# First 46 chunks of a gated recurrence scanned channel-major through TensorE transposes, all token loads issued by SyncE

## The chip, the cores and the metric

The kernel runs on one core of a Trainium2 chip. The metric is device time in microseconds (us), the median of its runs. Five engines work side by side, each through its own instructions in order: TensorE (PE, matmuls), VectorE (DVE), ScalarE (ACT), GpSimd (POOL) and SyncE (SP). SP, ACT and POOL also issue DMA transfers from their instruction streams; an engine whose next instruction is a transfer that must wait stands still until that wait is over. Sixteen DMA engines carry the transfers.

## The reference

Two stages follow each other. The first is a recurrence over 5056 time steps for 4 batch rows and 256 channels; the second sends each of the 20224 resulting rows (tokens) through one of 8 experts, chosen by a hash of the token's id.

```python
f = lower_bound + (1.0 - lower_bound) * sigmoid(f_logit)
i = 1.0 - f
for t in range(S):                       # S = 5056
    h = f[:, t] * h + i[:, t] * x[:, t]  # per batch row and channel
    y[:, t] = h
expert_idx = token_ids * 2654435761 % 8
for e in range(8):
    out[expert_idx == e] = relu(y[expert_idx == e] @ w1[e]) @ w2[e]   # 256 -> 1024 -> 256
```

## The kernel before, in words

**Chunks and blocks.** Time is cut into 158 chunks of 32 steps; a chunk holds 4 x 32 = 128 tokens. Chunks are grouped into 17 blocks (`NGS`: 2, 2, 4, eleven blocks of 12, then 8, 6, 4). For each block the program loads `f_t` and `x_t` (time on partitions, 256 channels along the row, 8 transfers, half of them issued by SP and half by ACT, line 479), takes the sigmoid (ACT, L503), turns both tiles with VectorE's 32x32 transpose so that time runs along the row (L530, tiles `sT` and `xT`), applies `lower_bound` (the gate, ACT, L544), forms the input term (DVE, L556), scans (DVE, L569, tile `y`) and turns the result back (DVE, L587, tile `yT`). A scan of one block starts from the last column of the block before.

**Routing.** A rank stage at the start computes for every token a place in a DRAM buffer `srt`, in which each expert has a contiguous region of 21 x 128 rows. GpSimd writes each chunk's 128 rows to their places by one indirect transfer (the scatter, L601): 158 scatters. GpSimd's transfers of the 16 weight tiles (L456, L458) stand among them.

**Experts.** 168 tiles of 128 rows (21 per expert) are read back turned (`xe`, an SP transfer, L680), multiplied by w1 (PE, 16 matmuls, L689), passed through relu (ACT, L698), multiplied by w2 (PE, 8 matmuls, L707), copied out of PSUM in pairs (ACT, L715, tile `ob`) and written to their token rows by an indirect GpSimd transfer (the out, L721): 168 outs. A tile may be read once every chunk that can hold one of its rows has been scattered. `window` bounds that from the statistics of the hash: 8 tiles become ready after block 3 (20 chunks), the last 8 after the last block. `Tab` (L620 to L659, DVE and PE) inverts the places into row numbers, which the outs need.

**What sets the order.** Nothing is scheduled on the chip. A planner in the program (`Plan`) gives each task an engine, a cost, a priority and dependencies, and emits a list; each engine then runs its part of the list in that order. Its priorities are due times in chunks (`due[k] = 6 + 2.3 * G0[k]`), a tile's is its last block's due time plus 30. A transfer issued by SP or ACT is given one of eight completion semaphores in turn (the names DMAHW0 to DMAHW7 in listings of the order), and before it is issued the engine waits until the transfer that had this semaphore before has landed, whichever queue that one is in. GpSimd's transfers have eight of their own (DMASW).

Of the kernel before, what the change touches and what calls it, by code (L numbers as in the profile page):

```python
# [15 lines left out]
P = 128  # L16
E = 8
# [27 lines left out]
class Task:  # L45
    def __init__(self, name, eng, prio, emit, deps=(), alloc=None, use=(), dma=0.0, lat=0.0, alt=False):
# [3 lines left out]
        self.done = None  # L50


class Plan:


    SEM = 0.12

# [13 lines left out]
    def order(self):  # L71
# [13 lines left out]
        def at(t):  # L85
            r = base[t]
# [11 lines left out]
        while left:  # L98
# [3 lines left out]
            for e in free:  # L102
# [25 lines left out]
            for c in kids.get(t, ()):  # L128
                base[c] = max(base.get(c, 0.0), t.done + self.SEM)
# [7 lines left out]
def kernel(  # L137
# [48 lines left out]
    ld = main.enter_context(tc.tile_pool(name="ld", bufs=2))  # L186
    sc = main.enter_context(tc.tile_pool(name="sc", bufs=2))
# [37 lines left out]
    def init_pool():  # L225
        nc.gpsimd.iota(i32a[:], pattern=[[1, NT]], base=0, channel_multiplier=0)
# [628 lines left out]
```

## Time and profile before

| | us |
|---|---|
| median of 2 runs | 620.59 (620.12 to 621.06) |
| span on the profile's page | 619.1 |
| a profiled execution as recorded: whole / its core's span | 616.68 / 614.9 |
| busy: PE, DVE, ACT, POOL | 348.5, 346.7, 321.1, 373.5 |
| HBM read and written | 58.49 MB, 33.95 MB |

Busy time is the time in which an engine executes; a GpSimd indirect transfer is counted while GpSimd makes it, not while it is under way. The two executions in the table differ: the one recorded took 1.8 us more than its core's span; with the same 1.8 us around it, the one on the page took 620.9 us. The trace is read by views: the page's summary, the waits of an engine, groups by line, stretches of time, and the timeline of one engine.

### The profile page before, as it was taken

The numbers are of one execution on the slowest core, as the hardware profiler recorded it, in microseconds if no ns is written. First come the engines' busy times: TensorE is split into PE (matmuls) and PEld (weight loads), VectorE is DVE, ScalarE is ACT, GpSimd is POOL, SyncE is SP. The second block draws the span as 40 slices with busy tenths as digits, with TensorE's granted clock in tenths as the row PEclk, the third lists the DMA queues.
The fourth block names the chain that finished last, engine by engine and source line by source line (L and its number), as shares of the span: only waits on it lengthen the run. The fifth ranks groups of instructions, "written<-read, shape, count | busy, mean of one in ns | idle before, by whom it ended". The sixth has DMA issues, their size and how long they took to land.

```text
span 619.1 us, 11412 instructions
## 1 busy us (share of the span) xinstructions
PE 348.5 (56%) x4258; PEld 320.1 (52%) x4258; DVE 346.7 (56%) x597; ACT 321.1 (52%) x431; POOL 373.5 (60%) x393
## 2 busy tenths in 40 slices
PE   2100005603696526289649975149870598986792
PEld 1000005503596426279638964149760597976792
DVE  8977989833993339988402777549539333110000
ACT  1333433703694517569418955058681377755372
POOL 6234374771277573887826776728777367776353
PEclk9999999956799758789968978559985598999697
DMA  8999999974048947843998387252883335333241
GB/s 154 274 264 288 231 230 154 261 209 90 26 121 200 291 97 143 214 95 109 207 231 187 90 174 138 64 102 79 195 214 96 89 92 153 113 105 95 80 100 54
DMA packets 116527, 94.58 MB, mean 153 GB/s; under 512 B 57133, under 2 KB 106801, under 8 KB 116468
## 3 DMA queue, kind: packets, MB, share of 16 engines
q0 software_dynamic: 23664, 39.61, 27.2%
q1 hardware_dynamic: 71114, 33.40, 24.3%
q10 hardware_dynamic: 21690, 20.79, 14.7%
q8 instruction: 35, 0.57, 0.4%
q14 instruction: 24, 0.20, 0.1%
HBM read 58.49 MB, written 33.95 MB: 149 GB/s over the span
## 4 chain that ended last, share of the span: by engine, by line
PE 27%; issue 24%; POOL 17%; DMA 16%; DVE 9%; ACT 4%; SPq 1%; ACTq 1%; POOLq 0%; DVEq 0%
PE hp L689 14%; PE op L707 13%; POOL srt L601 9%; POOL out_dram L721 8%; DMA xe<-srt 8%; DMA srt<-yT,pos_i 4%; DMA x_t<-in_x_dram 3%; ACT hT L698 2%; DVE y L569 2%; DVE xT L556 1%; DVE xT L530 1%; DVE sT L530 1%; ACT sT L544 1%; SPq L680 1%; DVE A L620 1%
## 5 line engine op out<-in xcount | busy, mean ns | idle before, releaser
L721 POOL DMA_INDIRECT out_dram<-ob,row_i x168 | 182.9, 1089 | 138.5 <-ACT ob L715 92.7
L689 PE MATMUL hp<-xe,w 128*128 128x128 bf16 x2688 | 197.6, 234 | 77.5 <-DMA xe<-srt 77.5
L601 POOL DMA_INDIRECT srt<-yT,pos_i x158 | 172.1, 1089 | 97.6 <-issue 44.8
L689 PEld LDWEIGHTS <-w 128*128 128x128 bf16 x2688 | 184.4, 106 | 84.4 <-issue 68.5
L698 ACT ACTIVATE hT<-hp 128x1024 bf16<-128x1024 f32 x168 | 170.2, 1022 | 110.9 <-PE hp L689 68.7
L707 PE MATMUL op<-w,hT 128*128 128x256 bf16 x1344 | 184.1, 285 | 64.1 <-ACT hT L698 63.9
L707 PEld LDWEIGHTS <-hT 128*128 128x128 bf16 x1344 | 129.4, 102 | 83.9 <-ACT hT L698 67.4
L544 ACT ACTIVATE sT<-sT,lb_col,c_col 128x384 f32<-128x384 f32 (+4 forms) x136 | 79.6, 629 | 117.3 <-DMA xe<-srt 56.0
L569 DVE TENSOR_TENSOR_SCAN y<-sT,y,xT 128x384 bf16<-128x384 f32 (+4 forms) x128 | 103.0, 845 | 0.5
L556 DVE SCALAR_TENSOR_TENSOR xT<-sT,xT 128x768 f32<-128x768 f32 (+2 forms) x58 | 50.0, 865 | 84.3 <-ACT sT L544 82.7
L530 DVE STREAM_TRANSPOSE xT<-x_t 128x768 f32<-128x768 f32 (+3 forms) x64 | 51.0, 808 | 46.9 <-DMA x_t<-in_x_dram 46.9
L640 PE MATMUL tp<-BP,A 128*128 128x64 bf16 (+4 forms) x158 | 9.4, 216 | 105.4 <-DVE BP L631 101.7
L503 ACT ACTIVATE f_t<-f_t 128x1024 f32<-128x1024 f32 (+1 forms) x41 | 40.3, 1017 | 51.8 <-DMA xe<-srt 25.0
L640 PEld LDWEIGHTS <-A 128*128 128x128 bf16 x158 | 8.4, 112 | 106.4 <-DVE A L620 80.0
L530 DVE STREAM_TRANSPOSE sT<-f_t 128x768 f32<-128x768 f32 (+3 forms) x64 | 50.7, 804 | 20.0 <-ACT f_t L503 18.2
L715 ACT COPY ob<-op 128x512 f32<-128x512 f32 x84 | 48.9, 582 | 5.0 <-PE op L707 4.9
L587 DVE STREAM_TRANSPOSE yT<-y 128x384 f32<-128x384 f32 (+4 forms) x68 | 30.3, 462 | 20.3 <-DMA srt<-yT,pos_i 20.0
L620 DVE TENSOR_TENSOR A<-iota_lo,lo_h 128x1536 bf16<-128x1536 bf16 (+4 forms) x17 | 23.4, 1374 | 0.0
L647 DVE TENSOR_TENSOR Tab<-Tab,tp 128x64 f32<-128x64 f32 (+4 forms) x17 | 3.3, 193 | 25.3 <-PE tp L640 25.1
L357 PE MATMUL rps<-cumI,onesb 128*128 128x8 bf16 (+2 forms) x24 | 3.7, 225 | 12.9 <-DVE cumI L342 12.3
L628 DVE TENSOR_TENSOR BP<-BP,v 128x384 bf16<-128x384 bf16 (+6 forms) x17 | 8.0, 472 | 0.6
L631 DVE TENSOR_TENSOR BP<-BP,v 128x384 bf16<-128x384 bf16 (+6 forms) x17 | 8.0, 471 | 0.6
(73 smaller groups left out, 81.0 us busy)
## 6 DMA issues: line engine op xcount, KB each, us to landing
f_t<-in_f_logit_dram SPq DMA_DIRECT2D x22, 384.0 KB
f_t<-in_f_logit_dram ACTq DMA_DIRECT2D x22, 384.0 KB
x_t<-in_x_dram ACTq DMA_DIRECT2D x22, 384.0 KB
x_t<-in_x_dram SPq DMA_DIRECT2D x22, 384.0 KB
w<-in_moe_w_dram POOLq DMA_DIRECT2D x16, 512.0 KB
xe<-srt SPq DMA_TRANSPOSE x168
out_dram<-ob,row_i POOLq DMA_INDIRECT x168
srt<-yT,pos_i POOLq DMA_INDIRECT x158
```

The lines of the kernel that those rows point to most:

```text
L503: nc.scalar.activation(v, v, AF.Sigmoid)
L530: nc.vector.transpose(o, i_)
L544: nc.scalar.activation(v, v, AF.Identity, scale=c_col[:, c:c + 1], bias=lb_col[:, c:c + 1])
L556: nc.vector.scalar_tensor_tensor(x_.rearrange("p s c l -> p (s c l)"), f_.rearrange("p s c l -> p (s c l)"), 1.0, x_.rearrange("p s c l -> ...
L569: nc.vector.tensor_tensor_scan(timed(T["y", k][:, cp, :L, s]), timed(T["sT", k, u][:, s, n, :]), timed(T["xT", k, u][:, s, n, :]), init, o ...
L587: nc.vector.transpose(T["yT", k].bitcast(FP32).rearrange("p m (c j) -> p c m j", j=32)[:, cp, :ng, :], T["y", k][:, cp, :L, :].rearrange(" ...
L601: bi = nc.gpsimd.indirect_dma_start(out=srt[:], out_offset=bass.IndirectOffsetOnAxis(ap=pos_i[:, g:g + 1], axis=0), in_=T["yT", k][:, m, : ...
L689: nc.tensor.matmul(hp[:, f, :], lhsT=w1_sb[e][:, h, f * P:(f + 1) * P], rhs=xe[:, h, :], start=(h == 0), stop=(h == 1),)
L698: nc.scalar.activation(hT[:], T["hp", j, e][:], AF.Relu)
L707: nc.tensor.matmul(op[:, h, :], lhsT=T["hT", j, e][:, f, :], rhs=w2_sb[e][:, f, :], start=(f == 0), stop=(f == FF - 1),)
L715: nc.scalar.copy(ob[:], T["op", n // 2][:])
L721: bi = nc.gpsimd.indirect_dma_start(out=out, out_offset=bass.IndirectOffsetOnAxis(ap=row_i[:, c:c + 1], axis=0), in_=T["ob", n // 2][:, h, ...
```

## The change

- **Blocks.** 24 blocks instead of 17: 2, 4, five of 8 chunks, then 4, 4, twelve of 8, 4, 2, 2 (`TS` in steps).
- **First 7 blocks (46 chunks) channel-major.** A load puts 128 tokens on partitions with 256 channels along the row, for a 256-step block two consecutive steps per partition. TensorE turns 128 x 128 pieces of `f_t` and `x_t` (float32, by an identity matrix) into PSUM, so that channels are on partitions; ACT takes the sigmoid from PSUM, then the gate; DVE forms the input term with `x` out of PSUM and scans; TensorE turns `y` (bfloat16) back and ACT copies it into `yT`. There are 184 float32 and 92 bfloat16 transposes of 128 x 128. No VectorE transposes are left in these blocks.
- **The other 112 chunks** keep the 32x32 layout. The state passes from one layout to the other by four matmuls and two VectorE instructions (`hand_pe`, `hand_dve`).
- **Queues.** All loads of `f_t` and `x_t` are issued by SP; ACT issues four loads of ids at the start only. Three blocks of loads are held instead of two (`XF`).
- **Weights** are released to GpSimd's order one every 4 us of the plan.
- **PSUM.** Two buffers instead of three for the first product (`hp`), four instead of two for the rest (`op`).
- **Planner.** It may take a task of better priority that becomes ready shortly after another (`LOOK`), the tables are due 25 later (`TABD`), the tiles are spread between blocks (`OFF`, `pace`).

The core of the diff:

```diff
-NGS = [2, 2, 4] + [12] * 11 + [8, 6, 4]
+TS = [64, 128] + [256] * 5 + [128, 128] + [256] * 12 + [128, 64, 64]
+KS = 7
+NGS = [t // 32 for t in TS]
-MID = 80
-RANGES = [(0, 8), (8, MID), (MID, NG)]
+RANGES = [(0, 6), (6, GA), (GA, MID), (MID, NG)]
+XF = 3
+OFF, TABD = 20.0, 25.0
+W0, W1 = 8.0, 4.0
...
+    LOOK = {"PE": 0.3, "ACT": 0.3, "DVE": 0.5, "POOL": 0.1, "SP": 0.1}
...
-                t = min((m[1] for m in mine if m[0] <= s + 1e-9), key=lambda t: t.prio)
+                s, t = min((m for m in mine if m[0] <= s + self.LOOK[e]), key=lambda m: (m[1].prio, m[0]))
...
-    pl.pool("hp", 3)
-    pl.pool("op", 2)
+    pl.pool("hp", 2)
+    pl.pool("op", 4)
...
-            weights.append(add(f"w{e}{v}", {"POOL": 0.85}, 14 + 2 * e + v, wl,
-                               [weights[-2]] if len(weights) >= 2 else [], dma=2.8, lat=2.0))
+            weights.append(add(f"w{e}{v}", {"POOL": 0.85}, 5, wl, rel=W0 + W1 * (2 * e + v), dma=2.8, lat=2.0))
...
+                nc.sync.dma_start(
+                    t[:, 2 * q * half:2 * q * half + 2 * q, :].rearrange("p (b r) d -> p b (r d)", r=q),
+                    src[2 * half:2 * half + 2].rearrange("b (p r) d -> p b (r d)", r=q),
+                )
...
+                    for n, view in enumerate(cview):
+                        nc.tensor.transpose(view(t), T[which, k][:, u * nch + n, h * P:(h + 1) * P], idf[:])
...
+                    nc.scalar.activation(
+                        T["sT", un][:, h * HS:h * HS + cols], T["tr", "f", uh][:, :cols], AF.Sigmoid
+                    )
...
+                        nc.tensor.transpose(t[:, n, h * P:(h + 1) * P], src, idn[:])
...
+            nc.tensor.matmul(
+                hp[:, c, :], lhsT=rep4[:, c].rearrange("p b j -> p (b j)"), rhs=last_y, start=True, stop=True
+            )
...
-            for b in (0, 2, 1, 3):
-                on_sp = b < 2
+            for b in range(B):
                 task = add(
-                    f"ld{t}{k}.{b}", {"SP": 0.45} if on_sp else {"ACT": 0.43}, pr - 12 if k > 1 else pr - 100,
-                    lambda t=t, b=b, q=nc.sync if on_sp else nc.scalar, f=load: f(t, b, q),
+                    f"ld{t}{k}.{b}", {"SP": 0.45}, pr - 22,
+                    lambda t=t, b=b, f=load: f(t, b, nc.sync),
...
-        pr = due[k] + 4
+        pr = due[k] + TABD
...
-        pr = due[lb] + 30 + 0.01 * n
+        mine = [i for i, t in enumerate(seq) if t[0] == lb]
+        pace = 2.3 * NGS[min(lb + 1, NB - 1)] / len(mine)
+        pr = due[lb] + 2.3 * NGS[lb] + OFF + pace * (n - mine[0])
```

**Order on ACT, the program before, around the loads of block 7 (chunks 56 to 67).** `f_t_1097` and `x_t_1096` are that block's loads, `sT` the gates of block 6; the brackets name what a row waits for.

```order
L503 ACTIVATE f_t_708<-f_t_708 128x1024 x2
L479 DMA f_t_1097<-in_f_logit_dram 32x12x256 [waits DMAHW4_49]
L479 DMA f_t_1097<-in_f_logit_dram 32x12x256 [waits DMAHW6_49]
L479 DMA x_t_1096<-in_x_dram 32x12x256 [waits DMAHW4_49,DVE_49]
L479 DMA x_t_1096<-in_x_dram 32x12x256 [waits DMAHW3_49]
L544 ACTIVATE sT_1136<-sT_1136,lb_col_86,c_col_87 128x384 [waits DVE_49]
```

On ACT in the changed program, where loads and sigmoids of the 32x32 blocks follow each other, at the sigmoid of block 10 (`hT` is a relu, `ob` a copy of a finished pair of tiles):

```order
L953 ACTIVATE hT_2106<-hp_2075 128x1024 [waits PE_49,Activation_49]
L797 ACTIVATE sT_2052<-sT_2052,lb_c_86,c_c_87 128x256
L756 ACTIVATE f_t_1653<-f_t_1653 128x1024 [waits DMAHW4_49,DMAHW5_49,DMAHW3_49,DMAHW2_49]
L970 COPY ob_2152<-op_2108 128x512 [waits DMASW7_49,DMASW6_49,PE_49]
L953 ACTIVATE hT_2174<-hp_2134 128x1024 [waits PE_49,Activation_49]
```

The transfers are gone from ACT; a wait on a DMAHW semaphore stands only before an instruction that uses what was loaded.

**Order on POOL in the program before, at the scatters of block 7 (`yT_1637`) and block 8 (`yT_2231`).** `srt<-yT` is a scatter, `out<-ob` an out, x11 a run of eleven.

```order
L601 DMA srt_79<-yT_1637,pos_i_88 21504x256 x10
L721 DMA out_0_dram<-ob_2369,row_i_90 20224x256 x2
L601 DMA srt_79<-yT_1637,pos_i_88 21504x256
L721 DMA out_0_dram<-ob_2440,row_i_90 20224x256 x2
L721 DMA out_0_dram<-ob_2516,row_i_90 20224x256 x2
L601 DMA srt_79<-yT_1637,pos_i_88 21504x256
L721 DMA out_0_dram<-ob_2574,row_i_90 20224x256 x2
L601 DMA srt_79<-yT_2231,pos_i_88 21504x256 x11
L721 DMA out_0_dram<-ob_2757,row_i_90 20224x256 x2
```

And in the changed program, at its blocks 13 (`yT_3569`) and 14 (`yT_3904`):

```order
L537 DMA srt_79<-yT_3569,pos_i_90 21504x256 x2
L976 DMA out_0_dram<-ob_4319,row_i_92 20224x256 x2
L537 DMA srt_79<-yT_3569,pos_i_90 21504x256
L976 DMA out_0_dram<-ob_4401,row_i_92 20224x256 x2
L537 DMA srt_79<-yT_3569,pos_i_90 21504x256
L537 DMA srt_79<-yT_3904,pos_i_90 21504x256
L976 DMA out_0_dram<-ob_4489,row_i_92 20224x256 x2
```

Runs of 10 to 16 scatters have become runs of one or two between pairs of outs; two longer runs are left, 24 before the first out and 11 near the end.

**Order on SP in the program before, at the end of the loads of block 7 and the tile reads (`xe`) behind them.**

```order
L479 DMA x_t_1096<-in_x_dram 32x12x256 [waits DMAHW5_49]
L680 DMA_TRANSPOSE xe_1179<-srt_79 128x2x128 [waits DMAHW7_49,DMASW7_49,PE_49]
L680 DMA_TRANSPOSE xe_1188<-srt_79 128x2x128 [waits DMAHW0_49,DMASW0_49,PE_49]
L680 DMA_TRANSPOSE xe_1197<-srt_79 128x2x128 [waits DMAHW1_49,DMASW1_49,PE_49]
L680 DMA_TRANSPOSE xe_1222<-srt_79 128x2x128 [waits DMAHW2_49,DMASW2_49,PE_49]
L680 DMA_TRANSPOSE xe_1246<-srt_79 128x2x128 [waits DMAHW3_49,DMASW3_49,PE_49]
```

And in the changed program, at the loads of block 12 (chunks 78 to 85):

```order
L935 DMA_TRANSPOSE xe_2182<-srt_79 128x2x128 [waits DMAHW5_49,PE_49]
L733 DMA f_t_2197<-in_f_logit_dram 32x8x256 [waits DMAHW6_49,DVE_49,Activation_49]
L733 DMA f_t_2197<-in_f_logit_dram 32x8x256 [waits DMAHW7_49]
L733 DMA f_t_2197<-in_f_logit_dram 32x8x256 [waits DMAHW0_49]
L733 DMA f_t_2197<-in_f_logit_dram 32x8x256 [waits DMAHW1_49]
L733 DMA x_t_2196<-in_x_dram 32x8x256 [waits DMAHW2_49,DVE_49]
```

Before, the last of block 7's loads on ACT and the read `xe_1246` on SP wait for the same semaphore, DMAHW3. Now the eight semaphores go round within one queue, and every load has reads ahead of it; here the reads ahead belong to tiles that need no chunk beyond 37.

## Rows read from the trace of the kernel before

**Rows 1.** The page's busy times: us, share of the span, instructions of each engine.

```profile
PE 348.5 (56%) x4258; PEld 320.1 (52%) x4258; DVE 346.7 (56%) x597; ACT 321.1 (52%) x431; POOL 373.5 (60%) x393
```

**Rows 2.** Groups by line on POOL, shapes apart: busy us, mean ns, idle before.

```profile
L721 POOL DMA_INDIRECT out_dram<-ob,row_i x168 | 182.9, 1089 | 138.5 <-ACT ob L715 92.7 <-issue 40.6 <-ACT hT L698 3.7
L601 POOL DMA_INDIRECT srt<-yT,pos_i x158 | 172.1, 1089 | 97.6 <-issue 44.8 <-DVE yT L587 34.6 <-DVE BP L628 16.0
```

**Rows 3.** Timeline of ACT: start, us, instruction, count, idle time before and releaser.

```profile
127.75 19.57 ACTq L479 DMA_DIRECT2D x_t<-in_x_dram  x2
147.36 2.50 ACT L544 ACTIVATE sT<-sT,lb_col,c_col 128x384 f32<-128x384 f32 x4 [24.56 <-DMA xe<-srt]
```

**Rows 4.** Chain of work that ended last, the same stretch: start, us, what.

```profile
143.49 3.49 DMA xe<-srt
```

**Rows 5.** Timeline of POOL: first outs after long gaps, last scatter.

```profile
165.53 2.21 POOL L721 DMA_INDIRECT out_dram<-ob,row_i  x1 [22.53 <-ACT ob L715]
...
242.34 1.57 POOL L721 DMA_INDIRECT out_dram<-ob,row_i  x1 [8.11 <-ACT ob L715]
...
326.50 0.98 POOL L721 DMA_INDIRECT out_dram<-ob,row_i  x1 [10.38 <-ACT ob L715]
...
417.79 1.50 POOL L721 DMA_INDIRECT out_dram<-ob,row_i  x1 [10.89 <-ACT ob L715]
...
495.38 0.98 POOL L721 DMA_INDIRECT out_dram<-ob,row_i  x1 [9.34 <-ACT ob L715]
...
576.55 0.98 POOL L601 DMA_INDIRECT srt<-yT,pos_i  x1 [0.31 <-issue]
```

**Rows 6.** The page's DMA issues: out<-in, queue, count, KB each.

```profile
f_t<-in_f_logit_dram SPq DMA_DIRECT2D x22, 384.0 KB
...
w<-in_moe_w_dram POOLq DMA_DIRECT2D x16, 512.0 KB
...
srt<-zero SPq DMA_DIRECT2D x1, 1536.0 KB
```

**Rows 7.** Stretches: engines' busy us (instructions), granted clock, DMA share, GB/s.

```profile
0.00:20.00 20.00, 4.27 (x66) 3.84 (x66) 16.63 (x53) 5.40 (x12) 9.38 (x56) 1.00 0.91 176
20.00:40.00 20.00, 1.26 (x18) 1.20 (x18) 18.19 (x65) 7.00 (x17) 8.58 (x8) 1.00 1.24 266
40.00:60.00 20.00, 0.00 (x0) 0.00 (x0) 13.19 (x24) 5.56 (x7) 7.27 (x8) 1.00 1.15 296
60.00:80.00 20.00, 0.00 (x0) 0.00 (x0) 19.55 (x31) 8.06 (x11) 7.12 (x6) 1.00 1.22 239
...
340.00:360.00 20.00, 20.00 (x280) 18.96 (x278) 16.02 (x22) 17.78 (x25) 15.61 (x14) 1.00 0.42 108
```

**Rows 8.** Groups by line, shapes apart, of the per-block work: busy us, mean ns.

```profile
L689 PE MATMUL hp<-xe,w 128*128 128x128 bf16 x2688 | 197.6, 234 | 77.5 <-DMA xe<-srt 77.5
...
L698 ACT ACTIVATE hT<-hp 128x1024 bf16<-128x1024 f32 x168 | 170.2, 1022 | 110.9 <-PE hp L689 68.7 <-DMA x_t<-in_x_dram 14.6 <-DMA xe<-srt 14.6
...
L556 DVE SCALAR_TENSOR_TENSOR xT<-sT,xT 128x512 f32<-128x512 f32 x10 | 6.7, 674 | 10.1 <-ACT sT L544 10.1
...
L569 DVE TENSOR_TENSOR_SCAN y<-sT,y,xT 128x256 bf16<-128x256 f32 x8 | 5.6, 729 | 0.0
...
L530 DVE STREAM_TRANSPOSE sT<-f_t 128x256 f32<-128x256 f32 x12 | 4.4, 410 | 1.3 <-DMA f_t<-in_f_logit_dram 1.3
L544 ACT ACTIVATE sT<-sT,lb_col,c_col 128x256 f32<-128x256 f32 x8 | 4.3, 590 | 4.9 <-DVE sT L530 4.8
...
L530 DVE STREAM_TRANSPOSE sT<-f_t 128x512 f32<-128x512 f32 x4 | 2.7, 682 | 0.0
...
L587 DVE STREAM_TRANSPOSE yT<-y 128x256 f32<-128x256 f32 x4 | 1.6, 409 | 0.0
```

**Rows 9.** Waits of SP's queue.

```profile
SPq L680 <- DMA srt<-yT,pos_i: 181.3, 39, 28.4
```

**Rows 10.** Waits of DVE.

```profile
DVE xT L530 <- DMA x_t<-in_x_dram: 46.9, 5, 24.6
```

More of the change, by code (lines that the diff above doesn't have):

```diff
@@ L262, in warm, with load_ids @@
     def warm():
         nc.scalar.activation(wrm[:], wrm[:], AF.Sigmoid)
-    def load_tok(q, b, part):
-        src = moe_token_ids[b * S:(b + 1) * S].rearrange("(g i) -> g i", i=32 * R)
-        n = NH - 1
+    def load_ids(k):
+        g, t, q = G0[k], T0[k], TS[k] // P
+        src = moe_token_ids.rearrange("(b s) -> b s", b=B)[:, t:t + TS[k]]
+        eng = nc.scalar if k < 4 else nc.gpsimd
+        with nc.allow_non_contiguous_dma(reason="8-byte ids"):
+            if q:
+                eng.dma_start(
+                    idt[:, g:g + NGS[k]].rearrange("p (b r) -> p b r", r=q), src.rearrange("b (p r) -> p b r", r=q)
+                )
+            else:
+                for h in range(2):
+                    eng.dma_start(
+                        idt[64 * h:64 * h + 64, g:g + 2], src.rearrange("(c h) i -> h i c", h=2)[h]
+                    )
@@ L302 @@
-    zf = add("fill", {"SP": 0.5}, -20, fill, [ip1], dma=4.5, lat=2.0)
-    ip2 = add("ip2", {"POOL": 7.0}, 20, init_pool2)
-    idv3 = add("idv3", {"DVE": 0.5}, 12, init_dve3, [ip])
-    tokl = []
-    for part in range(2):
-        for b in range(B):
-            on_sp = b < 2
-            tokl.append(add(
-                f"tok{part}{b}", {"SP": 0.45} if on_sp else {"ACT": 0.45}, -90 + part,
-                (lambda q, b, part: lambda: load_tok(q, b, part))(nc.sync if on_sp else nc.scalar, b, part),
-                [idv], dma=0.2, lat=2.0,
-            ))
@@ new lines @@
+    lbc = add("lbc", {"DVE": 0.1}, 40, lbc_dve, [lbcl])
+    lbd = add("lbd", {"DVE": 0.1}, -95, lb_dve, [lbl])
+    idl = {}
+    for k in range(KS):
+        idl[k] = add(f"ids{k}", {"ACT" if k < 4 else "POOL": 1.2 if TS[k] > 64 else 1.4},
+                     k - 105 if k < 4 else k - 99.5, lambda k=k: load_ids(k), dma=0.6, lat=2.0)
+    tokl = [add(f"tok{b}", {"SP": 0.45}, -30, lambda b=b: load_tok(b, 0), dma=0.4, lat=2.0) for b in range(B)]
+    if NA % 32:
+        tokl += [add(f"tok{b}", {"SP": 0.45}, -30, lambda b=b: load_tok(b, 1), dma=0.2, lat=2.0) for b in range(B)]
@@ L469 @@
+    ends = [t for t in pl.users[("y", KS - 1)] if t.name.startswith("sc")]
+    hpe = add("hpe", {"PE": 0.6}, due[KS] - 1, hand_pe, ends + [idv4], alloc=("op", "hand"), use=[("y", KS - 1)])
+    hdv = add("hdv", {"DVE": 0.3}, due[KS] - 1, hand_dve, [hpe], use=[("op", "hand")])
+    for k in range(KS, NB):
         ng = NGS[k]
```

479 lines of the change are left out of this document (337 added, 142 removed).

## The prediction, written before the changed kernel ran

> **What bounds the kernel now.** I read the busy times first: no engine is busy over 60% of the span, GpSimd most [rows 1]. So some engine waits in order, and the groups by line of GpSimd say how much. Its 326 indirect transfers (158 scatters, 168 outs) take 172.1 + 182.9 = 355.0 us, and between them lie 44.8 + 40.6 = 85.4 us that wait for nothing the profile shows [rows 2]. That is (355.0 + 85.4) / 326 = 1.351 us for each, 440 us in all, work that no order of the program shortens. The rest of GpSimd's time is waiting: 92.7 us in outs for ACT's copy `ob`, 34.6 us in scatters for `yT` and 16.0 us for the first scatter [rows 2]; what is left is setup and the end.
>
> Two mechanisms make the 92.7 us. First, **ACT stands behind a load**. ACT's timeline shows two loads of x that take from 127.75 to 147.3, and the gate behind them idle for 24.56 us before it [rows 3]; the chain of waits shows a tile read on SP landing at 143.49 + 3.49 = 146.98, the moment the load goes out [rows 4]. The load on ACT waits for the semaphore of a read on SP, that read waits for scatters, and meanwhile ACT does no relu. GpSimd's longest wait, 22.53 us at 165.53, follows at once; I put the 10.38 us at 326.50 to the same cause, 33 us together [rows 5]. Second, **outs stand too close behind their scatters**. Counting GpSimd's order, the first outs that need block 6, 10, 12 or 14 come 11 transfers after that block's last scatter. Those of the first three wait: 8.11, 10.89 and 9.34 us [rows 5]. So a scatter needs 11 x 1.351 + 9.4 = 24.3 us to become an out.
>
> **The sum.** GpSimd's queue is the frame: start, transfers, waits, tail, without overlap.
>
> *Start, until the first out may go.* The changed order has 49 scatters and the 16 weights ahead of the first out, and ACT's order has every sigmoid of the channel-major blocks ahead of the first relu, so no tile is computed while these blocks run. Bytes: a chunk is 384 KB / 12 x 2 x 4 = 256 KB of f and x; four loads of 384 KB make one block of 12 of each [rows 6], so 50 chunks are 13.1 MB. Weights 8.4 MB, the zero fill 1.6 MB [rows 6], the scatters of 46 chunks at 64 KB 3.0 MB; together 26.1 MB. The first 20 us moved 176 GB/s, or 3.5 MB, and the next three stretches 266, 296 and 239 at a DMA share above 1 [rows 7]; at their mean of 267 the other 22.6 MB take 85 us. With 3 us for the last block's way through the engines the first out stands at 108 us. Bounds: 96 us at 296 GB/s throughout. Upwards, the trace has no TensorE transposes. Nearest from below, PE's matmul of the same shape in bfloat16 is 234 ns, from the stretch at 340: 280 matmuls in 20 us are issued every 71 ns [rows 7], and 276 transposes at that pace are 20 us. From above, the VectorE transpose they replace takes 410 ns for 256 float32 columns [rows 8]; 276 of these are 113 us, and after 18 us of setup the start would be 131. I take 108, nearer to the DMA rows, because PE is nearly idle there now (at most 4.27 of 20 us) [rows 7].
>
> *The engines in that start.* VectorE loses the three transposes of 46 chunks. Per chunk it keeps an input term (at most 410 to 674 ns for half to all of a 512-wide tile) and a scan of 729 ns [rows 8], some 1.2 us; ACT has two instructions near 590 ns and half a copy, 1.4 us. Both stay under the 1.9 us per chunk that DMA allows, so I price the lighter VectorE at nothing. Its cover is the loads; were they faster it would count, which is in the lower bound.
>
> *Transfers.* From the first out to the last scatter the order has 263 transfers: 263 x 1.351 = 355 us. At 0.98 us plus the 0.31 of the quiet stretches [rows 5] it is 339.
>
> *Waits.* ACT issues no late loads any more, so its 33 us go. In the new order the first out of a block stands 24 to 47 transfers after its last scatter up to block 17 (18 in two cases), above the 24.3 / 1.351 = 18 that are needed. It is 10, 11, 14 and 15 for blocks 18 to 21: 24.3 less 1.351 for each gives 10.8 + 9.4 + 5.4 + 4.0 = 30 us. What is late next is the feed of chunks. In a block of 8, VectorE has 8 transposes of 682 ns, 4 input terms of 674, 8 scans of 729 and 4 transposes back of 409, 15.6 us [rows 8], with some 3.5 us of tables 19 us; ACT has 8 gates of 590, 8.5 relus of 1022 [rows 8] and the sigmoids and copies, 18 us; PE 8.5 tiles x 24 x 71 ns = 15 us. GpSimd's 16.5 transfers take 22 us. It stays last, but VectorE at 85% has little room: the smaller blocks raise work per chunk on VectorE and ACT. Bounds: 0, and the 92.7 us of today.
>
> *Tail.* The last scatter starts at 576.55 [rows 5] and the span ends 42.6 us later, with 16 outs behind it; in the new order there are 16 too. Bound below: 8 tiles less, 8 x 24 x 71 ns = 14 us.
>
> Handover, ids and iotas: each a few instructions under 1 us in the start, behind the loads.
>
> Sum: 108 + 355.3 + 29.6 + 42.6 = 535.5 us of span, against 619.1. With 1.8 us around the span, as in the recorded execution, the page's would be 620.9, 0.3 above the median, so I forecast **537 us**.
>
> **A rule on queues.** "DMA: Bandwidth & Descriptors", section "Issuing engines are not separate DMA queues", in the Trainium skill says that transfers of SP, ACT and GpSimd run on the same 16 engines and that the issuing engine only saves sequencer time. By that rule alone the move of loads to SP gains nothing and the sum would be 570; by the row, where ACT stood 24.56 us behind a load, 536. The page speaks of bandwidth, the row of who stands still, so I keep the row.
>
> **The rivals.**
>
> - *TensorE sets the start* (14%). For it: 276 transposes and their PSUM copies stand in a chain with ACT and VectorE, through four PSUM buffers. Against it: PE's pace above. At 131 instead of 108: 560 us. "TensorE: Matmul & The Clock Gate", section "Part 4: PE-mode transpose", in the Trainium skill gives about 390 ns for a bfloat16 128x128 transpose in isolation; by that figure I estimate 108 us of transposes and about 555 us; no row shows one.
> - *The waits stay* (11%): VectorE at 85%, and only two `hp` buffers between PE and ACT, make chunks and copies late, and GpSimd waits 92.7 us as now: about 600 us, some 7 less since a part of that lies in the tail.
> - *The slack is perfect* (10%): no waits and 1.29 us per transfer: 108 + 339 + 43 + 2 = 492 us; with a shorter tail less.
> - *SP becomes the queue that stops all* (4%), the one on the slower side. SP's reads wait 181.3 us for scatters [rows 9], and now all loads stand behind reads. Today VectorE waited 46.9 us in 5 times for x [rows 10], 9.4 each. If 12 of the 16 blocks of the 32x32 layout lose that: 537 + 113 = 650. It decides when the reads ahead of a load need chunks less than about 16 behind it. Counting SP's order the distance is 32 to 40 chunks, where it was 24 to 36, and that speaks against it.
> - The remaining 61% is my forecast. That the move does nothing is covered by the 570 above, inside the forecast's and second rival's spread.
>
> **The numbers.** Forecast 537 us. The forecast's own spread, 505 to 575, comes from the start (96 to 131) and the waits. The range reaches to 498 and 588, which takes in the first rival, a part of the third and nearly half of the second; about 7% lies below, 12% above. Two runs differ by under 1 us, so 2% (12.4 us) is the least that I call a change. Faster by over 2% (under 608.2): 0.91, all but the fourth rival and a part of the second; within 2%: 0.05; slower: 0.04.
>
> **What would show it.** GpSimd's first out near 108 us after 49 scatters. Waits of outs for `ob` near 30 us in place of 92.7, all after block 17. No idle time of ACT behind a transfer after the first microseconds. The last scatter near 493 us. PE busy more evenly, since it is fed in pairs. The forecast is wrong if the loads' rate in the first 100 us is not near 267 GB/s, if scatters wait for `yT` in the middle (VectorE is then the bound), or if `x_t` is waited for behind reads on SP.

## The result, and the profile after

The changed kernel takes **534.38 us** (median of 2 runs, 533.98 to 534.77) against 620.59: a ratio of 0.861 (0.857 to 0.865). The forecast was 537. The profiled execution has a span of 533.0 us.

Busy times of the kernel after, from its page (the same columns as [rows 1]):

```profile
PE 401.2 (75%) x4571; PEld 342.2 (64%) x4571; DVE 344.9 (65%) x799; ACT 353.6 (66%) x534; POOL 359.3 (67%) x426
```

In 86 us less, TensorE and ACT work 52.7 and 32.5 us more than before, VectorE and GpSimd 1.8 and 14.2 less. GpSimd's groups, which answer to [rows 2] (busy, mean ns, idle before and what ended most of it):

```profile
L976 POOL DMA_INDIRECT out_dram<-ob,row_i x168 | 172.5, 1027 | 75.4 <-issue 37.8 <-ACT ob L970 28.6 <-ACT hT L953 5.2
L537 POOL DMA_INDIRECT srt<-yT,pos_i x158 | 162.8, 1030 | 78.0 <-issue 38.4 <-DMA w<-in_moe_w_dram 22.3 <-DVE yT L843 6.7
...
L526 POOL DMA_DIRECT2D w<-in_moe_w_dram x8 | 6.0, 744 | 9.1 <-DMA w<-in_moe_w_dram 9.1
```

Waits for `ob` fell from 92.7 to 28.6 us, a transfer costs (172.5 + 162.8 + 37.8 + 38.4) / 326 = 1.262 us instead of 1.351, and there is a wait that the kernel before hardly had (0.5 us): GpSimd stands 22.3 + 9.1 = 31.4 us until its own weight transfers (`w`) land. GpSimd's timeline, at the places of [rows 5] (start, length, idle before):

```profile
89.49 1.00 POOL L537 DMA_INDIRECT srt<-yT,pos_i  x1 [4.04 <-DMA w<-in_moe_w_dram]
...
119.95 0.98 POOL L537 DMA_INDIRECT srt<-yT,pos_i  x1 [0.30 <-issue]
121.23 1.11 POOL L976 DMA_INDIRECT out_dram<-ob,row_i  x1 [0.30 <-DMA srt<-yT,pos_i]
...
156.60 1.15 POOL L537 DMA_INDIRECT srt<-yT,pos_i  x1 [6.34 <-DVE yT L843]
...
301.85 1.41 POOL L976 DMA_INDIRECT out_dram<-ob,row_i  x1 [3.69 <-ACT ob L970]
...
380.69 0.98 POOL L976 DMA_INDIRECT out_dram<-ob,row_i  x1 [5.72 <-ACT ob L970]
...
469.13 0.98 POOL L976 DMA_INDIRECT out_dram<-ob,row_i  x1 [2.04 <-ACT ob L970]
...
497.08 0.98 POOL L537 DMA_INDIRECT srt<-yT,pos_i  x1 [0.30 <-issue]
```

The first out goes at 121.23 after 46 scatters, the last scatter at 497.08. From 89.49 to 121.23 GpSimd runs 24 scatters one after the other, 0.30 us apart, and waits for nothing: their rows had been ready, GpSimd was late. The stretches of the start (as [rows 7]):

```profile
20.00:40.00 20.00, 6.57 (x78) 4.63 (x76) 10.17 (x24) 4.52 (x10) 6.49 (x54) 0.50 1.17 287
40.00:60.00 20.00, 10.06 (x71) 7.62 (x71) 17.84 (x51) 7.63 (x17) 10.41 (x12) 0.59 1.22 287
60.00:80.00 20.00, 15.07 (x88) 11.00 (x88) 19.10 (x50) 13.40 (x29) 9.15 (x10) 0.59 1.18 275
80.00:100.00 20.00, 15.22 (x88) 10.05 (x87) 18.84 (x45) 14.68 (x32) 13.22 (x13) 0.67 0.88 182
```

All transfers together run at 275 to 287 GB/s and thin out after 80 us. VectorE (third figure) is busy 55.8 of the 60 us from 40 to 100. The granted clock is 0.50 to 0.67 there. VectorE's timeline shows why so little comes out between 20 and 40:

```profile
33.48 0.45 DVE L395 TENSOR_SCALAR tlow<-tok 128x128 int32<-128x128 int32 x1 [6.73 <-DMA tok<-in_moe_token_ids_dram]
...
41.40 0.28 DVE L434 TENSOR_TENSOR tmp<-OH,rps 128x128 f32<-128x128 bf16 x1 [3.87 <-issue]
```

and ACT's (line 686 copies channel-major rows to `yT`):

```profile
24.57 0.59 ACT L686 COPY yT<-yp 128x512 bf16<-128x512 bf16 x1 [0.66 <-PE yp L672]
...
48.30 0.59 ACT L686 COPY yT<-yp 128x512 bf16<-128x512 bf16 x1 [21.74 <-PE tp L892]
...
70.62 0.59 ACT L686 COPY yT<-yp 128x512 bf16<-128x512 bf16 x1 [0.67 <-PE yp L672]
...
107.73 0.59 ACT L686 COPY yT<-yp 128x512 bf16<-128x512 bf16 x1 [0.89 <-PE yp L672]
```

For 24 us no chunk is finished, while VectorE does the ranks of late chunks and stands for ids. One such copy holds two chunks; the one at 70.62 is the twelfth, chunks 22 and 23, and the scatter of chunk 22 is the one at 89.49, 18 us after its rows were there.

### The profile page after: what moved, and what is told of

Read it like the earlier page. It is cut to its first block, busy times and chain, and to the rows that moved or that the text cites. A ratio compares the mean times of both kernels' runs of the same rounds, so it can differ in the third digit from the quotient of the medians.

```text
span 533.0 us, 12517 instructions
## 1 busy us (share of the span) xinstructions
PE 401.2 (75%) x4571; PEld 342.2 (64%) x4571; DVE 344.9 (65%) x799; ACT 353.6 (66%) x534; POOL 359.3 (67%) x426
## 5 line engine op out<-in xcount | busy, mean ns | idle before, releaser
L976 POOL DMA_INDIRECT out_dram<-ob,row_i x168 | 172.5, 1027 | 75.4 <-issue 37.8
L537 POOL DMA_INDIRECT srt<-yT,pos_i x158 | 162.8, 1030 | 78.0 <-issue 38.4
L826 DVE TENSOR_TENSOR_SCAN y<-sT,y,xT 128x256 bf16<-128x256 f32 (+2 forms) x128 | 77.7, 656 | 1.8
L797 ACT ACTIVATE sT<-sT,lb_c,c_c 128x256 f32<-128x256 f32 (+2 forms) x136 | 70.7, 561 | 4.2 <-DVE sT L783 3.2
L809 DVE SCALAR_TENSOR_TENSOR xT<-sT,xT 128x512 f32<-128x512 f32 x56 | 38.1, 680 | 45.6 <-ACT sT L797 45.0
L843 DVE STREAM_TRANSPOSE yT<-y 128x256 f32<-128x256 f32 (+2 forms) x68 | 24.6, 384 | 43.4 <-DMA srt<-yT,pos_i 30.5
L756 ACT ACTIVATE f_t<-f_t 128x1024 f32<-128x1024 f32 (+1 forms) x29 | 29.3, 1026 | 19.5 <-DMA f_t<-in_f_logit_dram 19.5
L783 DVE STREAM_TRANSPOSE xT<-x_t 128x512 f32<-128x512 f32 (+1 forms) x64 | 38.2, 607 | 2.0 <-DMA x_t<-in_x_dram 2.0
L783 DVE STREAM_TRANSPOSE sT<-f_t 128x512 f32<-128x512 f32 (+1 forms) x64 | 38.5, 613 | 0.3 <-issue 0.2
L636 DVE TENSOR_TENSOR_SCAN y<-sT,y,xT 128x256 bf16<-128x256 f32 (+1 forms) x48 | 33.6, 706 | 1.5
L602 PE MATMUL tf<-idf,f_t 128*128 128x128 f32 x92 | 27.1, 401 | 7.4 <-DMA f_t<-in_f_logit_dram 5.9
L602 PE MATMUL tx<-idf,x_t 128*128 128x128 f32 x92 | 26.5, 388 | 6.0 <-ACT yT L686 2.3
L614 ACT ACTIVATE sT<-sT,lb_col,c_col 128x256 f32<-128x256 f32 x46 | 27.6, 601 | 1.1
L875 DVE TENSOR_TENSOR A<-iota_lo,lo_h 128x512 bf16<-128x512 bf16 (+1 forms) x41 | 26.2, 640 | 0.0
```

The lines of the kernel that those rows point to most:

```text
L537: bi = nc.gpsimd.indirect_dma_start(out=srt[:], out_offset=bass.IndirectOffsetOnAxis(ap=pos_i[:, G0[k] + m:G0[k] + m + 1], axis=0), in_=T[ ...
L602: nc.tensor.transpose(view(t), T[which, k][:, u * nch + n, h * P:(h + 1) * P], idf[:])
L636: nc.vector.tensor_tensor_scan(yv[:, h, b, :tt], T["sT", un][:, c], T["vT", un][:, c], init, op0=ALU.mult, op1=ALU.subtract,)
L783: nc.vector.transpose(o, i_)
L797: nc.scalar.activation(v, v, AF.Identity, scale=c_c[:, c:c + 1], bias=lb_c[:, c:c + 1])
L809: nc.vector.scalar_tensor_tensor(x_.rearrange("p s c l -> p (s c l)"), f_.rearrange("p s c l -> p (s c l)"), 1.0, x_.rearrange("p s c l -> ...
```

## The experiments

Eight of the twelve runs, the group under the last heading of this section, ran where TensorE's results came late in every profile and the program before took 693 to 707 us; of those only the starts, and ratios among themselves, are used. The four told first ran with the program before at 613 to 618 us. By the record the eight ran on three chips and the four on two others, so chip and time cannot be told apart.

### Only the queue: the program before with its loads on SP (b_spn)

```diff
             for b in (0, 2, 1, 3):
-                on_sp = b < 2
+                on_sp = True
```

> The program before with all its loads of f and x issued by SP and nothing else, once more, with the program before at 613 us. Theory: ACT's standing behind loads goes and with it 33 us, some 580 to 588 us, a ratio of 0.945 to 0.96 (0.954 was measured while TensorE's results came late). Rival 1 (the issuing engine is nothing): a ratio of 0.99 to 1.01. Rival 2 (SP stands with loads behind reads): above 1.0.

Measured: 581.34 us against 617.75, a ratio of 0.943 (0.933 to 0.952). GpSimd's groups:

```profile
L721 POOL DMA_INDIRECT out_dram<-ob,row_i x168 | 177.8, 1058 | 98.0 <-ACT ob L715 54.8 <-issue 40.0 <-ACT hT L698 2.1
L601 POOL DMA_INDIRECT srt<-yT,pos_i x158 | 177.3, 1122 | 99.2 <-issue 46.2 <-DVE yT L587 35.4 <-DMA srt<-zero 16.4
```

Waits for `ob` fell by 37.9 us, to 54.8, and the span by 39.3; the scatters' waits are those of [rows 2]. So the queue is 36 us of the 86, as the theory had it. The planner, given other costs, also shifts GpSimd's order by a few places (26 scatters ahead of the first out, not 27). Loads of f do come later: ACT's sigmoid waits 46.6 us for them, 17.7 before. But VectorE waits 40.1 us for x where it was 46.9 [rows 10], and the time falls. The first outs that stood 11 or 12 transfers behind their scatters came to 8 to 11 us of waiting [rows 5] in three places; here are the first outs of the same blocks (6, 10 and 12):

```profile
222.97 0.98 POOL L721 DMA_INDIRECT out_dram<-ob,row_i  x1 [0.47 <-ACT ob L715]
...
388.86 1.35 POOL L721 DMA_INDIRECT out_dram<-ob,row_i  x1 [0.30 <-issue]
...
460.08 0.98 POOL L721 DMA_INDIRECT out_dram<-ob,row_i  x1 [2.50 <-issue]
```

They wait 0.5, 0.3 and 2.5 us at distances of 11, 11 and 12. The short distance was not what they had waited for. In the kernel before, ACT had stood behind a load shortly ahead of each of the three outs, at 242.34, 417.79 and 495.38 [rows 5], as it had in [rows 3]. Its loads of x go out at 227.68, 400.73 and 483.39, and these are the first instructions behind them (ACT's timeline; as in [rows 4], the stand ends with a tile read on SP):

```profile
229.36 1.30 ACT L544 ACTIVATE sT<-sT,lb_col,c_col 128x384 f32<-128x384 f32 x2 [16.20 <-DMA xe<-srt]
...
406.08 2.95 ACT L503 ACTIVATE f_t<-f_t 128x1024 f32<-128x1024 f32 x3 [25.04 <-DMA xe<-srt]
...
487.24 0.98 ACT L544 ACTIVATE sT<-sT,lb_col,c_col 128x192 f32<-128x192 f32 x2 [15.28 <-DMA xe<-srt]
```

Of the 54.8 us of waits that are left, 15 lie behind the last scatter; what makes the others was not traced.

### Only the due times: the changed program with the old ones (a_duen)

```diff
-OFF, TABD = 20.0, 25.0
+OFF, TABD = 20.0, 4.0
...
-        pr = due[lb] + 2.3 * NGS[lb] + OFF + pace * (n - mine[0])
+        pr = due[lb] + 30 + 0.01 * n
```

> The changed program with the old due times of tiles and tables, once more. Theory (the distance of an out behind its scatter costs 24.3 - 1.28 d, and 8 outs more in the tail cost 10 us): about 570 us where the changed program has 534, waits of outs for ob near 55 us, nearly all from block 14 on. Rival (distance does not matter, the feed does): 530 to 544 us, and waits for ob spread as before.

Measured: 552.28 us, a ratio of 0.891 (0.884 to 0.898), 18 us more than the changed program. That is in neither range, and not where the theory put it (waits for `ob` are 24.9 us, not near 55):

```profile
456.61 0.98 POOL L976 DMA_INDIRECT out_dram<-ob,row_i  x1 [1.16 <-ACT ob L970]
...
495.63 0.98 POOL L537 DMA_INDIRECT srt<-yT,pos_i  x1 [0.30 <-issue]
500.85 0.98 POOL L976 DMA_INDIRECT out_dram<-ob,row_i  x1 [4.24 <-ACT ob L970]
...
504.39 0.98 POOL L976 DMA_INDIRECT out_dram<-ob,row_i  x1 [1.27 <-ACT ob L970]
...
507.92 0.98 POOL L976 DMA_INDIRECT out_dram<-ob,row_i  x1 [1.26 <-ACT ob L970]
```

The last scatter goes at 495.63, as in the changed program (497.08), although the first out goes only at 174.01, after 65 scatters, 53 us later than there. A distance of 11 (at 456.61, 15.7 us after its block's last scatter) costs 1.2 us. The whole loss is the tail: 550.5 - 495.63 = 54.9 us instead of 533.0 - 497.08 = 35.9. Behind the last scatter a pair of outs goes every 3.53 us (500.85, 504.39, 507.92), set by TensorE and ACT, not every 2.6 us as GpSimd could; of the 19.0 us, four pairs more are 14.1, and the first pair waits 4.24 instead of 1.25, 3.0 more.

### Half of the transposes away (a_half)

```diff
                     for n, view in enumerate(cview):
-                        nc.tensor.transpose(view(t), T[which, k][:, u * nch + n, h * P:(h + 1) * P], idf[:])
+                        if n and cols > P:
+                            continue
+                        nc.tensor.transpose(
+                            t[:, :P] if cols > P else view(t), T[which, k][:, u * nch + n, h * P:(h + 1) * P], idf[:]
+                        )
...
```

The rest of the edit lets the sigmoid and the input term read the piece that is left twice, so the values of these chunks are wrong.

> The changed program with half of the float32 transposes of the 256-column units left out (the sigmoid and the input term read one 128 x 128 piece twice, so the values of these chunks are others); the order of all other instructions is the same. It takes away up to some 25 us of TensorE's work in the first 107 us, out of 73.7 us busy in the first 120. Read in the first 108 us, which were the same to 1.3 us in two runs of the changed program. Theory (VectorE's hole, VectorE's work after it and GpSimd's standing behind weights set the start): the last copy of a channel-major block into yT, at 107.7 us, moves by less than 3 us, and GpSimd's 46th scatter, at 119.95 us, by less than 3 us. Rival (TensorE with its transposes at the lower clock sets the start): both move forward by 10 to 25 us.

Measured: 529.57 us in a single run, beside 613.26 of the program before, a ratio of 0.864. The last copy to `yT` and the first out:

```profile
106.43 0.58 ACT L692 COPY yT<-yp 128x512 bf16<-128x512 bf16 x1 [0.89 <-PE yp L678]
```

```profile
121.22 0.98 POOL L982 DMA_INDIRECT out_dram<-ob,row_i  x1 [0.30 <-issue]
```

1.3 us and 0.01 us earlier. TensorE's busy time in the first 108 us fell from 62.1 to 53.7 us, so the edit took away 8.4 us and not up to 25; the copy followed by 1.3. TensorE does not set the start, though a transpose is dear and the clock low:

```profile
L602 PE MATMUL tx<-idf,x_t 128*128 128x128 f32 x74 | 21.7, 395 | 3.8 <-ACT sT L607 1.3 <-DVE Tab L899 1.1 <-ACT yT L686 1.0
L602 PE MATMUL tf<-idf,f_t 128*128 128x128 f32 x72 | 21.7, 409 | 1.5 <-DVE xT L621 0.4 <-ACT sT L607 0.4 <-ACT yT L686 0.3
```

(the changed program, groups by line on TensorE from 20 to 108 us). Transposes overlap: these 146 keep TensorE busy for 43.4 us, 0.30 each.

### A better start: late ranks, wider weights (a_st0n)

```diff
-        pr = (-60, 1, 15, 29)[ri]
+        pr = (-60, 1, 45, 52)[ri]
...
-    zfd = add("zfd", {"DVE": 0.1}, 5, filled, [zf])
+    zfd = add("zfd", {"DVE": 0.1}, 44, filled, [zf])
...
-    r0a = add("ra9", {"DVE": 0.8}, 13, rank_0a, tokl + [idv])
+    r0a = add("ra9", {"DVE": 0.8}, 44.5, rank_0a, tokl + [idv])
...
-    lbc = add("lbc", {"DVE": 0.1}, 40, lbc_dve, [lbcl])
+    lbc = add("lbc", {"DVE": 0.1}, 75, lbc_dve, [lbcl])
...
-W0, W1 = 8.0, 4.0
+W0, W1 = 8.0, 5.0
```

> The kernel with the three moves at the start (late ranks, late second coefficients, weights every 5 us) once more, now that the program before takes 613 us again. Theory A (VectorE's hole, then GpSimd's standing behind weights, set the start): first out near 104 us instead of 121.2; 17 us earlier, less 9 us for the seven scatters that come after it instead of before it, gives 8 us, and the waits for weights that go below 20 us: 520 to 528 us against 534. Theory B (the start costs nothing, since GpSimd catches up later or tiles cannot feed it): 532 to 540.

Measured: 533.35 us, a ratio of 0.863 (0.856 to 0.870): the changed program's time within the interval, as theory B has it. The start did get faster, and the time was given back at once:

```profile
101.48 0.98 POOL L976 DMA_INDIRECT out_dram<-ob,row_i  x1 [0.30 <-DMA srt<-yT,pos_i]
...
125.51 0.98 POOL L537 DMA_INDIRECT srt<-yT,pos_i  x1 [5.00 <-DVE yT L843]
...
133.45 0.98 POOL L537 DMA_INDIRECT srt<-yT,pos_i  x1 [2.79 <-DVE yT L843]
...
150.77 0.98 POOL L537 DMA_INDIRECT srt<-yT,pos_i  x1 [12.30 <-DVE yT L843]
...
170.81 0.98 POOL L537 DMA_INDIRECT srt<-yT,pos_i  x1 [9.60 <-DVE flv L513]
...
495.31 0.98 POOL L537 DMA_INDIRECT srt<-yT,pos_i  x1 [0.30 <-issue]
```

The first out is 19.8 us earlier, and scatters then wait 29.7 us for the feed of chunks 46 to 62, where the changed program waits 6.3. (`flv` is only the instruction behind the last `yT` of that block on VectorE, which ended at 170.53.) At 171 us GpSimd is at its 71st transfer, in the changed program at its 79th. In part the edit itself makes the feed late: the first tiles now stand ahead of the last 8 channel-major chunks on TensorE and ACT, so that TensorE stands for a tile read:

```profile
88.35 1.86 PE L944 MATMUL hp<-xe,w 128*128 128x128 bf16 x16 [4.14 <-DMA xe<-srt]
```

The copies into `yT`, 2 to 5 us apart from 50 us on, come at 83.81, 94.22 and 107.07 there. So the run shows that an early first out alone is worth nothing; what a start without that price would be worth, it does not show. No run that computes everything beats the changed program by more than about 1 us.

### The runs with late results

(b_sp, a_act, a_due, a_rank; then a_same, a_st0, a_ks4; then a_st0r.) b_sp, a_due, a_st0 and a_st0r are the kernels b_spn, a_duen and a_st0n above. The other edits, each to the changed program (a_rank has the ranks' and the fill's lines of a_st0n only, a_same none):

```diff
# a_act
-                    f"ld{t}{k}.{b}", {"SP": 0.45}, pr - 22,
-                    lambda t=t, b=b, f=load: f(t, b, nc.sync),
+                    f"ld{t}{k}.{b}", {"SP": 0.45} if b < 2 else {"ACT": 0.43}, pr - 22,
+                    lambda t=t, b=b, f=load: f(t, b, nc.sync if b < 2 else nc.scalar),
# a_ks4
-KS = 7
+KS = 4
```

| run | us | ratio to the program before |
|---|---|---|
| b_sp | 662.73 | 0.954 (0.947 to 0.961) |
| a_act | 692.97 | 0.996 (0.992 to 1.001) |
| a_due | 683.31 | 0.982 (0.974 to 0.990) |
| a_rank | 671.35 | 0.965 (0.957 to 0.973) |
| a_same | 690.56 | 0.978 (0.969 to 0.987) |
| a_st0 | 699.56 | 0.994 (0.989 to 0.998) |
| a_ks4 | 694.09 | 0.988 (0.980 to 0.995) |
| a_st0r | 689.33 | 0.996 (0.991 to 1.001) |

a_same: 

> The changed program itself, unchanged, run beside the ones below and beside the program before, since the program before took 693 us on the chip of the first four runs where it had taken 621. If that chip only stretches everything, the ratio to the program before is near 0.861 and the ratios of the first four runs can be read beside it. If it costs a fixed amount of idle time on TensorE and ACT, both lose some 70 us and the ratio is (534 + 70) / (621 + 70) = 0.874. If it costs time in proportion to how closely the engines work, the changed program loses more and the ratio is above 0.90.

The same program, so its trace can be laid beside the one above. Stretches of a_same, then ACT's largest wait (us in all, times, longest):

```profile
80.00:100.00 20.00, 15.05 (x93) 10.31 (x91) 18.97 (x46) 14.38 (x32) 14.00 (x13) 0.67 0.89 182
100.00:120.00 20.00, 3.19 (x17) 2.09 (x16) 4.39 (x11) 3.24 (x7) 12.54 (x14) 0.50 0.51 145
```

```profile
ACT hT L953 <- remote: 101.7, 30, 6.2
```

Up to 100 us the two agree. After that ACT stood 30 times, 101.7 us in all, ahead of a relu of a product of TensorE; "remote" says that the profile knows no releaser, and VectorE has such waits too (31.5 us). What held them stays open. No such row is in the traces of the program before, of the changed program's first run or of the four runs above. GpSimd's queue is then no longer the frame, so whole times say nothing of the theories; the starts do.

a_rank: 

> The changed program with the ranks of chunks 46 and up, and the wait for the zero fill, some 30 to 40 us later in VectorE's order. In the changed program VectorE stood 6.73 us for the ids and 3.87 us for the fill between 26 and 42 us, no chunk was finished from 25 to 46 us, and VectorE was then busy without a gap to 107. Theory A (VectorE's feed sets the start): that hole goes, and the first out comes at 100 to 111 us instead of 121. Theory B (GpSimd's waits for the semaphores of the weights set it): the first out stays at 121, less 4 us for three scatters fewer ahead of it. Theory C (PE's transposes at the lower clock set it): stays at 121 too, with PE busy without a gap. The planner also puts the first outs of blocks 9 to 11 only 14 to 15 transfers behind their scatters, which by the distance rule costs 17 us, so the whole time is 520 to 540 by A, 545 to 555 by B and C.

Its first out came at 120.17, after a stop of the kind above (VectorE 9.88 us at 104.89), so it decides nothing. Its rank work moved as meant: VectorE has no such wait for ids any more. But it then stood for the second copy of the coefficients, which a_st0 moves as well:

```profile
44.12 0.17 DVE L365 TENSOR_SCALAR c_c<-lb_c 128x8 f32<-128x8 f32 x1 [7.58 <-DMA lb_c<-in_lower_bound_dram]
```

Before the stop, the copy of chunks 34 and 35 came at 89.52, in the changed program at 91.31: theory A's hole alone is worth 1.8 us there.

a_st0: 

> The changed program with three things moved at its start and nothing else: ranks of chunks 46 and up and the wait for the fill later on VectorE, the second copy of lower_bound's coefficients later on VectorE, and weights every 5 us instead of 4 on GpSimd. GpSimd's order has 39 scatters ahead of the first out instead of 46, the distances stay at 20 and more up to block 17, and behind the last scatter are 16 outs as before. Theory A (VectorE's hole from 25 to 46 us and then GpSimd's standing behind weights set the start): the first out comes at 95 to 105 us instead of 121, GpSimd's waits for weights fall from 31 to below 15 us, and the whole time falls by 10 to 20 us. Theory B (DMA sets the start, all loads and weights must land): the first out comes 9 us earlier for the seven scatters fewer, but scatters later wait for yT, and the whole time stays within 4 us of the changed program's.

First out at 104.48, which is theory A's; waits for weights 19.6 us instead of 31.4, more than the 15 expected. The whole time said nothing.

a_st0r: 

> The same kernel as in the run before with the three moves at the start, again, since in the runs so far TensorE's results came 2 to 6 us late some 30 times from 100 us on, in every kernel (the changed program itself took 691 us there instead of 534, and its first 100 us were the same to 1.3 us). If those stops are gone, the program before takes about 621 us, and by theory A (VectorE's hole, then GpSimd's standing behind weights, set the start) this kernel takes 515 to 525 us: the first out stood at 104.5 us instead of 121.2, 17 us earlier, seven scatters less are ahead of it and come later (9 us), and the slack after it takes some back. By theory B (DMA sets it) 530 to 538 us. If the stops are still there, both take about 700 us and nothing follows from the whole time.

The late results were still there; nothing followed.

b_sp: 

> The program before, with the loads of f and x that ACT issued moved to SP; nothing else. Theory (GpSimd's queue is the frame, ACT stood behind loads): the 33 us that GpSimd lost while ACT stood behind a load go, and the outs still stand 11 transfers behind their scatters, so waits for ob fall from 92.7 to about 60 us and the time to about 588 us. Rival 1 (the new layout and the new order made the gain, the queue is nothing): 620 us, and ACT's idle time only moves to another wait. Rival 2 (SP now stands with loads behind its reads): over 620 us, and VectorE's waits for x_t grow far above 46.9 us.

The ratio, 0.954, has the theory's (588 / 621 = 0.947) at the edge of its interval, and agrees with b_spn. The waits for `ob` say nothing here: they are 138.5 us, with the late results in them.

a_due: 

> The changed program with the old due times of tiles and tables. GpSimd's order has 65 scatters before the first out, distances of 25 and more up to block 13, then 12, 12, 26, 16, 11, 14, 9, 13, 17, and 24 outs behind the last scatter instead of 16. Theory (distance rule 24.3 - 1.28 d, and the tail): waits 59 us by the rule where the changed program has 33, so 26 more, and 8 outs more in the tail, 10 us: about 570 us. Rival (distance is not what makes outs wait; PE, ACT and VectorE feed at their own pace): within 10 us of 534.

a_act: 

> The changed program, with half of the loads of the 32x32 blocks issued by ACT again; the planner then also orders GpSimd anew, and the first outs of blocks 11 to 15 stand 13 to 22 transfers behind their scatters, those of blocks 18 to 23 9 to 12. Theory: ACT stands behind loads again (about 33 us of GpSimd's waits), and a distance d below 19 costs 24.3 - 1.28 d, some 66 us in all where the changed program has 33 by the same rule: 534 + 33 + 33 = about 600 us, at least 565. Rival (the layout makes the gain, or the issuing engine is nothing): within 10 us of 534.

a_ks4: 

> The changed program with 4 channel-major blocks (22 chunks) instead of 7 (46 chunks); the blocks, queues and due times stay. GpSimd's order then has first outs 13 to 17 transfers behind their scatters in blocks 11 to 15, 9 to 13 in blocks 17 to 21, and 24 outs behind the last scatter. Theory (GpSimd's order is what counts): by the rule 24.3 - 1.28 d the waits are 74 us where the changed program has 33, and 8 outs more in the tail cost 10: 51 us more than the changed program, of which 10 for scatters that precede the first out come back: some 575 where the changed program has 534, a ratio of 1.08. Rival (the layout itself is the gain, through VectorE's transposes of 24 chunks): VectorE gets 24 x 2.2 us = 53 us of transposes back in the start, the first out comes at 140 to 170 us, and the ratio is 1.05 to 1.10 too; the two differ in the place, the first out's time against the waits for ob after it.

For these three the late results cover what was asked. a_due was run again above; for a_act and a_ks4 it stays open what half the loads on ACT cost in the new order, and what 24 channel-major chunks less cost. For that, a_ks4 has one hint: its first out stood at 125.89 after 38 scatters, where the expectation for the layout was 140 to 170, and beside it a_same's at 128.38 after 46; 694.09 and 690.56 us are within each other's spread. So the layout of those 24 chunks shows no gain there.

## Why the prediction was right, point by point

**The frame held.** Start, transfers, waits and tail of GpSimd's queue: 108 + 355 + 30 + 43 were forecast; measured are 121.2 to the first out, 375.8 from there to the last scatter, and 35.9. The sum is right within 3 us because errors of either sign met (+13, -9 and -7 us); that is luck.

**Start, 13 us short.** The transfers were faster than I had them: 231 GB/s in the first 20 us against 176, then 275 to 287 against 267; by the page's slices they run at 242 GB/s up to 93 us and at 81 behind that, where the sum has 105. The step that failed is "I price the lighter VectorE at nothing. Its cover is the loads". The loads were no cover: from 55 us on no transpose waits for one, and SP stood in them until TensorE gave a buffer back (us in all, times, longest):

```profile
SPq L560 <- PE tf L602: 18.6, 3, 12.5
```

Per chunk I counted 1.2 us of VectorE and left out tables and ranks. From 46 to 107 us VectorE was busy for 57.5 of 61 us, 1.7 for each of 36 chunks, behind a hole in which it stood for ids and for the fill. That VectorE set the feed is read from this and was not shown by a run. The last rows were in `yT` at 108.3, by luck the 108 that I had for the first out, with the loads as the cause.

The 13 us on top of that are GpSimd's, for whose own queue the start had no term: it stood 31.4 us until weights landed, was 18 us behind the rows at 89.49, and then ran 24 scatters back to back. And a_st0n and a_duen show that the first out's time is no price by itself: 19.8 us earlier changed the whole by 1, and 53 us later did not move the last scatter.

**Transfers, too dear.** 1.262 us where I took 1.351; my lower bound was 1.29. The busy part fell from 1089 to 1027 and 1030 ns. Loads on SP alone did not do it (1058 and 1122 in b_spn); what did was not tried.

**Waits, right in size by luck and wrong in place.** 28.6 us against 30, but 6.7 of them lie in the tail, which the sum counts apart, and only the 1.7 and 3.3 us of blocks 18 and 19 are where I put them. The other 17 come before block 18, where I had none. The step that failed is the second mechanism, "outs stand too close behind their scatters", and its 24.3 us: at distances of 10 and 11 an out needs 14.3 and 15.9 us from its block's last scatter in the changed program (437.84 - 423.54 in block 18, 469.13 - 453.26 in block 19). The 24.3 was read from three outs ahead of which ACT had stood behind a load as well, 16.20, 25.04 and 15.28 us; I had looked for that only at 165.53 and 326.50. In b_spn, with the distances unchanged, they wait 0.3 to 2.5 us. So of the 92.7 us the first mechanism carried 37.9 net, not 33, and the distance little.

The waits in the middle have another cause. The three longest, 2.60 us at 254.84, 3.69 at 301.85 and 5.72 at 380.69, follow waits of ACT for a load of f (6.57, 4.56 and 5.50 us), the last of them here:

```profile
374.60 0.63 ACT L756 ACTIVATE f_t<-f_t 128x512 f32<-128x512 f32 x1 [5.50 <-DMA f_t<-in_f_logit_dram]
```

ACT no longer issues loads, but its sigmoid still stands in line ahead of the relus; such waits sum to 19.5 us in 6 places. The prediction's sign "no idle time of ACT behind a transfer" failed with that.

**Tail, 7 us shorter.** 16 outs in both; the first pair waited 7.42 us before and 1.25 now, which is nearly all of it. a_duen gives the price of a pair, 3.53 us.

**The rule on queues.** "DMA: Bandwidth & Descriptors", section "Issuing engines are not separate DMA queues", in the Trainium skill has an issuing engine save only sequencer time. That the bandwidth is shared agrees with the trace: with one engine issuing the loads it is 275 to 287 GB/s between 20 and 80 us, with two it was 239 to 296 [rows 7]. For the time the measurement decides: moving the issue of half the loads off ACT gave 36 us, because ACT had stood for the waits of the transfers it issued, 24.56 us for one pair [rows 3].

**The rivals.** TensorE sets the start: a_half speaks against it. My price for the transposes was wrong all the same: the 276 keep TensorE busy for 27.1 + 26.5 + 16.8 = 70.4 us (`f_t`, `x_t`, `y`), where I had 20 from the nearest row. A float32 transpose takes 395 to 409 ns in the groups above, a bfloat16 one 292. The figure of "TensorE: Matmul & The Clock Gate", section "Part 4: PE-mode transpose", in the Trainium skill (390 ns, for bfloat16 in isolation) was near the float32 rows; the 108 us that I estimated from it were too long since transposes overlap, and the 555 us since they also run beside loads and VectorE. The granted clock is 0.50 to 0.67 while transposes make up most of TensorE's work, from the lower level (1.2 GHz) to a mixture of both, and that is part of the price: a pair of float32 transposes takes 0.63 to 0.69 us from 66 to 70 us, at 0.50, and 0.44 from 70.4 to 73 us, at 1.00. (In the first 12 us the profile shows 1.00 while a pair takes 0.63 to 0.69, so the level shown there is not to be relied on.) SP becomes the queue that stops all: VectorE waited 2.0 us for `x_t`, not 46.9 [rows 10], and SP 115.3 us for scatters instead of 181.3 [rows 9]. The waits did not stay, and the slack was not perfect, though the transfers cost even less than the 1.29 us of that rival. Two counts in the prediction are off, without weight: 46 scatters and not 49 stand ahead of the first out (the 263 transfers behind it are right), and the 32x32 layout has 17 blocks, not 16.

**What the 86 us are.** The queue 36 to 39 (b_spn). The rest, 46.8 us of span between b_spn and the changed program, shows in GpSimd's groups as shorter transfers (19.8 us of busy time, 10.0 of issue), 26.2 of `ob`, 28.7 of VectorE's `yT` and 16.4 of the zero fill, less 31.4 for the weights and 5.0 for ACT's copies into `yT`; the remaining 18 us the other way are short gaps with other names and setup. Which part of the change each belongs to, the layout, the blocks, three-deep buffers, PSUM or the planner's order, was not separated, so the cause of these 47 us stays open; that the layout, which names the change, has a share in them is not shown.

## What to carry to other kernels

Here an engine that both computes and issues transfers stood for the waits of those transfers, and that was worth 36 us. Look for idle time of such an engine that ends with a DMA, and move the issue to one that only issues. When a delay is calibrated on waits, take only places where the engine between was free, or two causes are counted as one. An earlier first result is not yet a faster start: lay the times at which the queue that frames the kernel reaches the same transfer side by side in both traces before paying for it.

## Seen of the hardware, not expected

- 43.4 us of float32 128 x 128 transposes on TensorE between 20 and 108 us, one every 0.30 us, where I had taken 71 ns as the nearest row; a pair took 0.63 to 0.69 us at a granted clock of 0.50 and 0.44 at 1.00.
- GpSimd stood 31.4 us for the landing of its own weight transfers of 512 KB while the DMA share was above 1; with one every 5 us of the plan instead of 4 it was 19.0.
- One and the same program took 534 and 691 us at different times and, by the record, perhaps on different chips, with its first 100 us equal to 1.3 us; the difference shows as late results of TensorE, and its cause is open.
